# A last block of 64 queries filled up to 128 rows in windowed attention with two layers behind it

## The chip, the cores and the metric

One NeuronCore of a Trainium2 chip runs the whole program. The metric is the device time of one execution in microseconds, the median of several runs. TensorE multiplies (a stationary operand is loaded by its weight loader, then a moving operand streams through), VectorE, ScalarE and GpSimd work on elements, and SyncE's queue issues the DMAs.

## The reference

```python
# q, k, v: (4, 8, 576, 64)
scores = q @ k.T / sqrt(64)
rel = pos[:, None] - pos[None, :]
mask = (rel >= 0) & (rel < 128)
scores = where(mask, scores - slopes[h] * abs(rel), -1e9)
attn = softmax(scores) @ v              # sum + 1e-9 in the division
x = attn, heads side by side            # 2304 tokens x 512
h = x @ w_in                            # 512 x 2048, float64 weights in 32-bit words
x = (h * clip(h + 3, 0, 6) / 6) @ w_out
h = maximum(x @ w_in2, 0)
out = (s * h * h + b) @ w_out2
```

A query sees the 128 keys up to its own, so a block of 128 queries meets its own block of keys and the one before. A sequence of 576 is four blocks of 128 and a last one of 64.

## The kernel before

The attention is cut into units: one head and a range of query blocks. Groups 0 and 1 are blocks 0 and 1 of batches 0 and 1, in full float32 (`StartUnit`). Groups 2 and 3 are blocks 0 and 1 of the other two batches, groups 4 to 7 are blocks 2, 3 and 4 of all batches (`Unit`); block 4 has 64 rows, `rows(4)`. So 4 groups x 8 heads = 32 units have three blocks, the last one short, and 48 units have two full blocks.

A `Unit` goes through these steps. `load` fetches the queries and keys, transposed. `casts` (ScalarE) and `rests` (VectorE) split the scaled queries into a high part X and a rest Y. `products` (line 312) multiplies, for each block, X and then Y as the stationary operand with the keys of both blocks: 256 moving columns for a full block, 192 for the short one, whose stationary operand has 64 columns. `minima` (lines 328, 329; VectorE) folds the two squares into one and takes row minima, `exps` (line 339; ScalarE) exponentiates with row sums, `sums` (lines 350, 356; VectorE) adds 1e-9 and takes reciprocals, for full blocks and the short one apart. `weights` (line 362; GpSimd) scales the rows. `transposes` (line 371; TensorE) turns each block; for the short one the operand has 64 rows. `fold` and `masks` (lines 377, 389) spread the result over both key blocks. `values` (line 404), for two heads at once, each in its half of the columns, multiplies by the values, one key block after the other; the short key block has 64 rows. `to_hi` and `to_lo` write the first layer's input.

Each layer runs in steps of 128 inner columns: h (line 574, 12 products) and later o (line 632 in the first layer, 12 products; line 646 in the second), with ScalarE and VectorE making g from h in between. Every step of everything has a slot and a rank in a plan written out by hand; each engine's program is that order. TensorE's slots alternate layer products with a piece of the attention, and the second layer's weights are decoded (lines 168 to 208) after the attention.

Buffers: X and Y come from tags with two buffers of 320 columns in the pool `ap`; the start units take their scaled queries from the same tags. The start units' raw data lie in tiles of the later weight buffers w8 to w11. `warm`, the operand of the warm-up products, is a constant tile.

```python
lhsT=x[:, q : q + rows(i)]                                      # products
self.pt[:, li * P : li * P + r], self.Pt[:r, li], ident[:r, :r] # transposes
lhsT=u.rv[: rows(j), j - self.ka], rhs=u.W[: rows(j), o : o + n]  # values
```

Of the kernel before, what the change touches and what calls it, by code (L numbers as in the profile page):

```python
# [22 lines left out]
def tile_alibi_window_attention_moe_moe2(  # L23
# [12 lines left out]
):  # L36
    """Every float32 product runs as float32r passes over an exact split x = hi + lo."""
    nc = tc.nc
# [24 lines left out]

# [1 line left out]
    # The tensor engine's program is cut in slots: in each, twelve or nine products of a layer and  # L65
    # a piece of the attention. Every other step has the slot in which its operands are there.
    plan = {}
# [15 lines left out]

# [1 line left out]
    # The tensor engine's clock doubles after some microseconds of work.  # L85
    warm = const.tile([P, 256], F32, name="warm")
    nc.vector.memset(warm, 0.0)
# [6 lines left out]
    ident = const.tile([P, P], F32, name="ident")  # L94
    # A query row r meets the columns c <= r of its own block and c > r of the block before, at
    # the distances r - c and 128 + r - c: as two squares (rel2) and as one of both (rel).
    own = const.tile([P, P], I32, name="own")
# [30 lines left out]
    def bank(name):  # L128
        """A PSUM bank of the attention: the accumulators' too while they are free."""
        nonlocal nbank  # L130
        free = 4 if slot < FIRST else 2 if slot < hslot[1, 0] else 0
        nbank += 1
        k = nbank % (3 + free)
        if k < free:
            return ps_o.tile([P, 512], F32, tag=f"o{3 - k}", name=name)
        return ps_w.tile([P, 512], F32, tag="a", bufs=3, name=name)

# [1 line left out]
    wt = {}  # L139

    class Half:
        """
        Half a block of weights: float64 words to float32, rounded to nearest, then split into
        float32r parts.
        """

# [25 lines left out]
        def high(self):  # L172
            # As float32 the high word has the exponent's bits 3 places low, and too large by 112.
            if self.stage is None:
# [37 lines left out]

# [1 line left out]
    bounds1 = [(b * S + qa * P, n) for (b, qa, _), n in zip(groups, SIZES1)]  # L214
# [14 lines left out]
    def rows(i):  # L229
        return min(P, S - i * P)  # L230

    class Unit:
        """The query blocks [qa, qb) of one head: keys from block qa - 1 on."""

# [45 lines left out]
        def casts(self):  # L280
            self.c = -(D ** -0.5) / slopes[self.h]
            self.X = ap.tile([P, 320], F32R, tag="X", name=f"X{self.id}")[:, : self.nq]
            self.C = ap.tile([P, 448], F32R, tag="C", name=f"C{self.id}")[:, : self.nk]
            nc.scalar.activation(self.X, self.rq, AF.Copy, scale=self.c)
            nc.scalar.activation(self.C, self.rk, AF.Copy)

        def rests(self):
            self.Y = ap.tile([P, 320], F32R, tag="Y", name=f"Y{self.id}")[:, : self.nq]
            nc.vector.scalar_tensor_tensor(
                out=self.Y, in0=self.rq, scalar=self.c, in1=self.X.bitcast(F32),  # L290
                op0=ALU.mult, op1=ALU.subtract,
            )
            nc.gpsimd.tensor_tensor(  # L293
                out=self.C[D:], in0=self.rk[D:], in1=self.C[D:].bitcast(F32), op=ALU.subtract
            )

        def square(self, i):
            o = (i - self.qa) % 2 * 256
            k0 = max(0, i - 1) * P
            k1 = min((i + 1) * P, S)  # L300
            return self.ps[(i - self.qa) // 2][: rows(i), o : o + k1 - k0], k0, k1

        def products(self, a, b):
# [4 lines left out]
            for i in range(a, b):  # L308
                sl, k0, k1 = self.square(i)
                q = (i - self.qa) * P  # L310
                for x in (self.X, self.Y):
                    nc.tensor.matmul(  # L312
                        sl,
                        lhsT=x[:, q : q + rows(i)],
                        rhs=self.C[:, k0 - self.ka * P : k1 - self.ka * P],
# [4 lines left out]
        def minima(self, a, b):  # L320
# [3 lines left out]
            for i in range(a, b):  # L324
                sl = self.square(i)[0]
                li, r = i - self.qa, rows(i)
                if i:
                    nc.vector.copy_predicated(out=sl[:, :r], mask=own[:r, :r], data=sl[:, P:])  # L328
                nc.vector.tensor_tensor_reduce(  # L329
                    out=self.Pt[:r, li], in0=sl[:, :P], in1=(rel if i else rel0)[:r],  # L330
                    scale=slopes[self.h], scalar=3.0e38, op0=ALU.add, op1=ALU.min,
                    accum_out=self.st[:r, 0, li : li + 1],
                )

        def exps(self, a, b):
            for i in range(a, b):
                li, r = i - self.qa, rows(i)
                pt = self.Pt[:r, li]
                nc.scalar.activation(  # L339
                    pt, pt, AF.Exp, bias=self.st[:r, 0, li : li + 1], scale=-1.0,  # L340
                    accum_out=self.st[:r, 1, li : li + 1],
                )

        def sums(self):
            nqb = self.qb - self.qa
            full = nqb if rows(self.qb - 1) == P else nqb - 1
            st = self.st
            for r, a, b in ((P, 0, full), (rows(self.qb - 1), full, nqb)):
                if a < b:
                    nc.vector.tensor_scalar(  # L350
                        out=st[:r, 2, a:b], in0=st[:r, 1, a:b], scalar1=1e-9, scalar2=None,
                        op0=ALU.add,
                    )
            for r, a, b in ((P, 0, full), (rows(self.qb - 1), full, nqb)):
                if a < b:
                    nc.vector.reciprocal(st[:r, 2, a:b], st[:r, 2, a:b])  # L356

        def weights(self):
            for i in range(self.qa, self.qb):
                li, r = i - self.qa, rows(i)  # L360
                pt = self.Pt[:r, li]
                nc.gpsimd.tensor_scalar(  # L362
                    out=pt, in0=pt, scalar1=self.st[:r, 2, li : li + 1], scalar2=1.0,
                    op0=ALU.mult, op1=ALU.mult,
                )

        def transposes(self):
            self.pt = bank(f"t{self.id}")
            for i in range(self.qa, self.qb):
                li, r = i - self.qa, rows(i)  # L370
                nc.tensor.transpose(  # L371
                    self.pt[:, li * P : li * P + r], self.Pt[:r, li], ident[:r, :r]
                )

# [4 lines left out]
        def masks(self):  # L379
            # Per query block: its weights for the key block before, then for its own.  # L380
            self.W = ap.tile([P, 640], F32, tag="W", bufs=4, name=f"W{self.id}")
# [12 lines left out]
        def values(self):  # L394
            """Of two heads: each in its half of the tensor engine's columns."""
            self.xr = bank(f"v{self.id}")[:, : self.nq]
            for j in range(self.ka, self.qb):
# [4 lines left out]
                for u in self.pair():  # L402
                    p = slice((u.h % 2) * D, (u.h % 2 + 1) * D)
                    nc.tensor.matmul(  # L404
                        self.xr[p, q0 : q0 + n],
                        lhsT=u.rv[: rows(j), j - self.ka],
                        rhs=u.W[: rows(j), o : o + n],
                        start=j == self.ka,
# [3 lines left out]

        # Two heads' outputs, transposed, into the tile of the first layer's input.
        def to_hi(self):
# [8 lines left out]
    class StartUnit(Unit):  # L423
        """Query blocks 0 and 1, in float32 products: while the tensor engine has little to do."""

# [15 lines left out]
        def load(self):  # L441
            j = self.b * H // 2 + self.h // 2
            if j % 2 == 0:
                raws[j // 2] = wpool.tile(
                    [P, 2, 768], F32, tag=f"w{j // 2 + 8}", name=f"raw{self.id}"
                )
            raw = raws[j // 2][:, j % 2]
            nc.sync.dma_start(out=raw, in_=qkv0p[self.b, self.h // 2])
            for u in self.pair():
                u.raw = raw  # L450
                u.p = slice((u.h % 2) * D, (u.h % 2 + 1) * D)
                u.rk = raw[u.p, 256:512]
                u.rv = raw[:, 512 + 2 * D * (u.h % 2) :].rearrange("p (n d) -> p n d", d=D)

        def scale(self):
            """Both heads' queries over the scale and the slope."""
            tag = "XY"[self.h // 4]
            X = ap.tile([P, 320], F32, tag=tag, name=f"X{self.id}")[:, :256]
            for u in self.pair():
                u.X = X[u.p]  # L460
                c = -(D ** -0.5) / slopes[u.h]
# [80 lines left out]

# [1 line left out]
    late = {}  # L544

    class Step:
        """One block of a layer's inner columns, for one tile of tokens."""

# [134 lines left out]
    class Input2:  # L683
        """A tile of the second layer's input."""

# [24 lines left out]

# [1 line left out]
    k = 0  # L712
# [92 lines left out]
```

## Time and profile before

| | |
|---|---|
| time, median of 3 runs | 983.91 us (981.29 to 985.71) |
| span of the profiled execution | 985.2 us |
| TensorE busy | 956.8 us (97%), 5978 products |
| weight loader busy | 867.5 us (88%) |
| VectorE, ScalarE, GpSimd busy | 550.0 (56%), 457.6 (46%), 307.6 us (31%) |
| granted TensorE clock | 1.000 |
| chain of work that ended last | TensorE 75%, VectorE 17%, issue 3%, DMA 3% |

The span runs from the first to the last instruction; no separate time of the profiled execution is given beside it. Products are pipelined and their ends are modelled, so a product's duration is a latency, and what a piece of the program costs is read from the start of one line to the start of the next. "issue" names idle time for which the profile shows nothing that was waited for.

### The profile page before, as it was taken

What the parts mean: (1) busy time and instruction counts of PE and PEld (TensorE: products, weight loads), DVE (VectorE), ACT (ScalarE), POOL (GpSimd) and SP (SyncE); (2) the same over time, 40 slices, a digit from 0 to 9 for tenths busy, and PEclk for the clock granted to TensorE, in tenths of its full rate; (3) what the DMA queues carried; (4) which work ended last, traced back from release to release, by engine and by line L of the source; (5) the groups of instructions that cost most, each with busy time, mean ns of one, the idle gap of its engine ahead of it and who ended that gap; (6) DMA issues with size and microseconds to landing.
All of it is one profiled execution on the core that took longest, in us unless ns stands there. A gap on an engine that the chain in (4) does not pass through costs nothing.

```text
span 985.2 us, 16371 instructions
## 1 busy us (share of the span) xinstructions
PE 956.8 (97%) x5978; PEld 867.5 (88%) x5978; DVE 550.0 (56%) x1398; ACT 457.6 (46%) x1185; POOL 307.6 (31%) x556
## 2 busy tenths in 40 slices
PE   8998889999999999999999899899999999999998
PEld 5687779999999999999999888799999999999997
DVE  5999996555565555555328999933333333323322
ACT  4767675455544445444327776632333323323322
POOL 5865885335554344434204543300000000000000
PEclk9999999999999999999999999999999999999999
DMA  6263552213212113112014563320010100200000
GB/s 238 83 199 113 156 161 66 87 62 106 71 60 92 44 59 98 59 45 70 1 50 151 163 207 124 110 65 1 1 65 1 62 3 0 65 1 1 33 1 33
DMA packets 34384, 73.93 MB, mean 75 GB/s; under 512 B 4352, under 2 KB 13568, under 8 KB 34304
## 3 DMA queue, kind: packets, MB, share of 16 engines
q1 hardware_dynamic: 34304, 72.89, 22.8%
q8 instruction: 47, 0.77, 0.3%
q14 instruction: 33, 0.27, 0.1%
HBM read 63.44 MB, written 9.44 MB: 74 GB/s over the span
## 4 chain that ended last, share of the span: by engine, by line
PE 75%; DVE 17%; issue 3%; DMA 3%; ACT 1%; POOL 1%; SPq 0%; POOLq 0%; ACTq 0%; DVEq 0%
PE h L574 33%; PE o L646 18%; PE o L632 16%; DVE w L208 4%; PE v L404 3%; PE s L312 2%; DVE zq L187 2%; PE t L371 2%; DVE g L611 2%; DMA stage<-w 2%; DVE stage L187 2%; DVE zq L190 1%; DVE stage L190 1%; DVE t L591 1%; PE s L477 1%
## 5 line engine op out<-in xcount | busy, mean ns | idle before, releaser
L574 PE MATMUL h<-x,w 128*128 128x384 f32 (+2 forms) x2688 | 447.2, 315 | 9.7 <-DVE t L591 9.7
L574 PEld LDWEIGHTS h<-x,w 128*128 128x128 f32 x2688 | 418.5, 190 | 21.3 <-DVE t L591 12.7
L587 ACT ACTIVATE t<-h 128x384 f32<-128x384 f32 (+2 forms) x224 | 99.5, 444 | 374.3 <-PE h L574 373.3
L632 PE MATMUL o<-g,w 128*128 128x256 f32 (+1 forms) x1536 | 231.9, 299 | 4.1 <-DVE g L611 2.8
L646 PE MATMUL o<-w,g 128*128 128x512 f32 x864 | 217.2, 395 | 4.3 <-ACT g L606 2.9
L632 PEld LDWEIGHTS o<-g,w 128*128 128x128 f32 x1536 | 210.0, 189 | 9.1 <-DVE g L611 4.2
L646 PEld LDWEIGHTS o<-w,g 128*128 128x128 f32 x864 | 159.8, 188 | 37.5 <-ACT g L606 5.5
L595 DVE SCALAR_TENSOR_TENSOR t<-t,s_sb 128x384 f32<-128x384 f32 x96 | 64.4, 671 | 171.6 <-ACT t L587 171.6
L389 POOL TENSOR_SCALAR_AFFINE_SELECT W<-F 128x128 f32<-128x128 f32 (+1 forms) x240 | 71.5, 337 | 142.9 <-ACT F L377 139.2
L591 DVE SCALAR_TENSOR_TENSOR t<-t,h 128x256 f32<-128x256 f32 (+1 forms) x128 | 57.3, 448 | 88.9 <-ACT t L587 88.9
L611 DVE TENSOR_TENSOR g<-t,g 128x256 fp32r<-128x256 f32 (+1 forms) x128 | 76.0, 594 | 41.4 <-ACT g L604 40.6
L613 DVE SCALAR_TENSOR_TENSOR g<-t,b_sb,g 128x384 fp32r<-128x384 f32 x96 | 65.1, 678 | 54.1 <-ACT g L606 54.0
L606 ACT ACTIVATE g<-t,b_sb 128x384 fp32r<-128x384 f32 x96 | 59.2, 616 | 63.4 <-DVE t L595 63.4
L196 POOL TENSOR_TENSOR zq<-zq 128x512 int32<-128x512 int32 x40 | 57.2, 1429 | 83.4 <-DVE zq L190 77.3
L604 ACT ACTIVATE g<-t 128x256 fp32r<-128x256 f32 (+1 forms) x128 | 56.0, 438 | 17.7 <-DVE t L591 16.9
L293 POOL TENSOR_TENSOR C<-raw,C 64x448 fp32r<-64x448 f32 (+1 forms) x48 | 49.6, 1033 | 41.9 <-issue 23.4
L362 POOL TENSOR_SCALAR P<-P,st 128x128 f32<-128x128 f32 x128 | 53.5, 434 | 7.8 <-DVE st L356 6.1
L339 ACT ACTIVATE P<-P,st 128x128 f32<-128x128 f32 x128 | 49.5, 390 | 0.0
L328 DVE COPY_PREDICATED s<-own,s 128x128 f32<-128x128 int32 (+1 forms) x112 | 30.5, 273 | 31.8 <-PE s L312 30.1
L196 POOL TENSOR_TENSOR stage<-stage 128x512 int32<-128x512 int32 x24 | 34.4, 1432 | 37.6 <-DVE stage L190 28.5
L329 DVE CUSTOM_DVE_ANT_0 P<-s,rel 128x128 f32<-128x128 f32 x128 | 36.8, 288 | 7.3
L208 DVE TENSOR_TENSOR w<-zq,w 128x512 fp32r<-128x512 f32 x40 | 37.5, 937 | 0.0
(74 smaller groups left out, 830.6 us busy)
## 6 DMA issues: line engine op xcount, KB each, us to landing
raw<-w SPq DMA_DIRECT2D x40, 512.0 KB, 5.0
stage<-w SPq DMA_DIRECT2D x24, 512.0 KB, 4.2
raw<-qk SPq DMA_DIRECT2D x32, 384.0 KB, 3.1
out<-y SPq DMA_DIRECT2D x18, 256.0 KB, 2.3
raw<-qk SPq DMA_DIRECT2D x16, 256.0 KB, 2.7
rv<-v SPq DMA_DIRECT2D x16, 256.0 KB, 3.4
raw<-qkv0p SPq DMA_DIRECT2D x8, 384.0 KB, 7.2
x2d<-y SPq DMA_DIRECT2D x8, 320.0 KB, 2.9
```

Source lines behind the costliest of these rows:

```text
L196: nc.gpsimd.tensor_tensor(out=self.q, in0=self.z, in1=self.q, op=ALU.add)
L208: nc.vector.tensor_tensor(out=w[:, 1, self.c], in0=self.q.bitcast(F32), in1=w[:, 0, self.c].bitcast(F32), op=ALU.subtract,)
L389: nc.gpsimd.affine_select(out=self.W[:, o : o + r], in_=self.F[:, q : q + r], fill=0.0, base=k - 1, compare_op=ALU.is_ge, pattern=[[s, r]] ...
L574: nc.tensor.matmul(self.ps, lhsT=w[:, wp, cc * P : (cc + 1) * P], rhs=x[:, cc, xp], start=m == 0, stop=m == 3 * CC - 1,)
L587: nc.scalar.activation(self.a, self.ps, AF.Relu, **bias)
L591: nc.vector.scalar_tensor_tensor(out=self.a, in0=self.a, scalar=6.0, in1=self.ps, op0=ALU.min, op1=ALU.mult)
L595: nc.vector.scalar_tensor_tensor(out=self.a, in0=self.a, scalar=s_sb, in1=self.a, op0=ALU.mult, op1=ALU.mult)
L606: nc.scalar.activation(self.g[:, 0], self.a, AF.Identity, bias=b_sb)
L611: nc.vector.tensor_tensor(out=self.g[:, 1], in0=self.a, in1=hi, op=ALU.subtract)
L613: nc.vector.scalar_tensor_tensor(out=self.g[:, 1], in0=self.a, scalar=b_sb, in1=hi, op0=ALU.add, op1=ALU.subtract,)
L632: nc.tensor.matmul(acc[t][d], lhsT=w[:, wp, DM + d * P : DM + (d + 1) * P], rhs=self.g[:, gp], start=f == 0 and i == 0 and (t > 1 or d % 2 ...
L646: nc.tensor.matmul(acc[t][tb], lhsT=self.g[:, gp, tb * P : (tb + 1) * P], rhs=w[:, wp, DM:], start=f == 0 and i == 0, stop=f == NF - 1 and ...
```

## The change

All instructions of the short block run over 128 rows or columns. The query tiles X and Y get 384 columns, of which the last 64 are set to zero once, at the start, by GpSimd; they are two fixed tiles each, used in turn. The scores of the 64 added rows come from zero queries, and their weights, minima and sums are never used: `fold` still copies 320 columns. The values' short key block multiplies 128 rows, the added ones being zero in the prepared values. `sums` needs two instructions in place of four. To make room, `warm` moves into the buffer w7 of the weights, and the start units' scaled queries move into the tile of their raw data (now 1024 columns per pair).

```diff
-    warm = const.tile([P, 256], F32, name="warm")
+    warm = wpool.tile([P, 256], F32, tag="w7", name="warm")
...
+    queries = {}
+    for x in "XY":
+        queries[x] = [ap.tile([P, 3 * P], F32R, tag=f"q{x}{i}", bufs=1, name=f"q{x}{i}") for i in (0, 1)]
+        for t in queries[x]:
+            nc.gpsimd.memset(t[:, S - 2 * P :].bitcast(F32), 0.0)
+
+    def query_tile(x):
+        queries[x].reverse()
+        return queries[x][0]
...
-            self.X = ap.tile([P, 320], F32R, tag="X", name=f"X{self.id}")[:, : self.nq]
+            self.X = query_tile("X")
...
-            nc.scalar.activation(self.X, self.rq, AF.Copy, scale=self.c)
+            nc.scalar.activation(self.X[:, : self.nq], self.rq, AF.Copy, scale=self.c)
...
-            return self.ps[(i - self.qa) // 2][: rows(i), o : o + k1 - k0], k0, k1
+            return self.ps[(i - self.qa) // 2][:, o : o + k1 - k0], k0, k1
...
-                        lhsT=x[:, q : q + rows(i)],
+                        lhsT=x[:, q : q + P],
...
-                    nc.vector.copy_predicated(out=sl[:, :r], mask=own[:r, :r], data=sl[:, P:])
+                    nc.vector.copy_predicated(out=sl[:, :r], mask=own[:, :r], data=sl[:, P:])
...
-                li, r = i - self.qa, rows(i)
-                pt = self.Pt[:r, li]
+                li = i - self.qa
+                pt = self.Pt[:, li]
...
-            for r, a, b in ((P, 0, full), (rows(self.qb - 1), full, nqb)):
-                if a < b:
-                    nc.vector.reciprocal(st[:r, 2, a:b], st[:r, 2, a:b])
+            nc.vector.reciprocal(st[:, 2, :n], st[:, 2, :n])
...
-                nc.tensor.transpose(
-                    self.pt[:, li * P : li * P + r], self.Pt[:r, li], ident[:r, :r]
-                )
+                nc.tensor.transpose(self.pt[:, li * P : (li + 1) * P], self.Pt[:, li], ident)
...
-                        lhsT=u.rv[: rows(j), j - self.ka],
-                        rhs=u.W[: rows(j), o : o + n],
+                        lhsT=u.rv[:, j - self.ka],
+                        rhs=u.W[:, o : o + n],
...
-                    [P, 2, 768], F32, tag=f"w{j // 2 + 8}", name=f"raw{self.id}"
+                    [P, 2, 1024], F32, tag=f"w{j // 2 + 8}", name=f"raw{self.id}"
...
-            nc.sync.dma_start(out=raw, in_=qkv0p[self.b, self.h // 2])
+            nc.sync.dma_start(out=raw[:, :768], in_=qkv0p[self.b, self.h // 2])
...
+                u.X = raw[u.p, 768:]
...
-            X = ap.tile([P, 320], F32, tag=tag, name=f"X{self.id}")[:, :256]
```

## Rows read from the trace of the kernel before

**Rows 1.** Stages: us, then each engine's busy us, clock, DMA share, GB/s.

```profile
core 0: us, PE busy (x) PEld busy (x) DVE busy (x) ACT busy (x) POOL busy (x), PEclk, DMA share, GB/s
...
40.00:155.00 115.00, 101.03 (x743) 90.19 (x743) 111.30 (x230) 79.99 (x202) 85.90 (x96) 1.00 0.46 144
...
208.00:497.00 289.00, 289.00 (x2179) 270.93 (x2178) 151.64 (x608) 135.47 (x448) 122.57 (x323) 1.00 0.20 63
497.00:523.00 26.00, 26.00 (x179) 26.00 (x178) 10.19 (x21) 9.68 (x21) 1.30 (x1) 1.00 0.31 105
523.00:640.00 117.00, 108.77 (x603) 97.53 (x601) 108.55 (x151) 79.07 (x154) 51.61 (x35) 1.00 0.44 146
```

**Rows 2.** TensorE's timeline among three-block units: start, us, instructions.

```profile
226.56 0.25 PE L312 MATMUL s<-C,X 128*64 128x192 f32 x1
226.65 0.25 PE L312 MATMUL s<-C,Y 128*64 128x192 f32 x1
226.74 0.58 PE L371 MATMUL t<-ident,P 128*128 128x128 f32 x3
227.25 1.70 PE L632 MATMUL o<-g,w 128*128 128x256 f32 x12
228.79 1.60 PE L574 MATMUL h<-x,w 128*128 128x256 f32 x12
...
249.42 1.46 PE L404 MATMUL v<-W,rv 128*64 128x128 f32 x16
250.81 0.64 PE L371 MATMUL t<-ident,P 128*128 128x128 f32 x3
251.38 1.69 PE L632 MATMUL o<-g,w 128*128 128x256 f32 x12
```

**Rows 3.** TensorE's timeline among two-block units.

```profile
198.15 0.38 PE L371 MATMUL t<-ident,P 128*128 128x128 f32 x2
198.29 1.68 PE L632 MATMUL o<-g,w 128*128 128x256 f32 x12
199.81 1.60 PE L574 MATMUL h<-x,w 128*128 128x256 f32 x12
201.25 0.23 PE L312 MATMUL s<-C,X 128*128 128x128 f32 x1
...
201.71 1.59 PE L632 MATMUL o<-g,w 128*128 128x256 f32 x12
...
204.67 0.87 PE L404 MATMUL v<-W,rv 128*64 128x256 f32 x8
205.47 0.44 PE L371 MATMUL t<-ident,P 128*128 128x128 f32 x2
205.66 1.67 PE L632 MATMUL o<-g,w 128*128 128x256 f32 x12
```

**Rows 4.** TensorE's timeline, three full transposes of a start unit.

```profile
53.95 0.49 PE L516 MATMUL t<-ident,P 128*128 128x128 f32 x3
54.19 0.48 PE L574 MATMUL h<-x,w 128*128 128x256 f32 x2
```

**Rows 5.** The weight loader's timeline; in brackets its idle time before.

```profile
306.17 0.13 PEld L371 LDWEIGHTS t<-ident,P 64*128 64x128 f32 x1 [0.17 <-issue]
...
315.37 0.20 PEld L404 LDWEIGHTS v<-W,rv 64*64 64x64 f32 x4 [0.28 <-issue]
```

**Rows 6.** Waits of the weight loader, 208 to 497 us: total, times, longest.

```profile
PEld t L371 <- issue: 5.5, 33, 0.2
PEld v L404 <- issue: 4.6, 17, 0.3
```

**Rows 7.** Groups by line and shape: count, busy us, mean ns.

```profile
L371 PE MATMUL t<-ident,P 64*128 64x64 f32 x32 | 8.7, 272 | 0.0
...
L350 DVE TENSOR_SCALAR st<-st 64x1 f32<-64x1 f32 x32 | 4.4, 137 | 0.0
```

**Rows 8.** GpSimd's timeline: one unit's weights.

```profile
309.62 1.06 POOL L362 TENSOR_SCALAR P<-P,st 128x128 f32<-128x128 f32 x3
```

**Rows 9.** Timeline of the start: VectorE's first use of a query.

```profile
6.86 0.61 DVE L463 TENSOR_SCALAR X<-raw 64x256 f32<-64x256 f32 x2 [4.24 <-DMA raw<-qkv0p]
```

More of the change, by code (lines that the diff above doesn't have):

```diff
@@ L281, in casts @@
             self.c = -(D ** -0.5) / slopes[self.h]
-            self.X = ap.tile([P, 320], F32R, tag="X", name=f"X{self.id}")[:, : self.nq]
+            self.X = query_tile("X")
             self.C = ap.tile([P, 448], F32R, tag="C", name=f"C{self.id}")[:, : self.nk]
-            nc.scalar.activation(self.X, self.rq, AF.Copy, scale=self.c)
+            nc.scalar.activation(self.X[:, : self.nq], self.rq, AF.Copy, scale=self.c)
             nc.scalar.activation(self.C, self.rk, AF.Copy)
         def rests(self):
-            self.Y = ap.tile([P, 320], F32R, tag="Y", name=f"Y{self.id}")[:, : self.nq]
+            self.Y = query_tile("Y")
             nc.vector.scalar_tensor_tensor(
-                out=self.Y, in0=self.rq, scalar=self.c, in1=self.X.bitcast(F32),
+                out=self.Y[:, : self.nq], in0=self.rq, scalar=self.c,
+                in1=self.X[:, : self.nq].bitcast(F32),
                 op0=ALU.mult, op1=ALU.subtract,
@@ L327, in minima @@
                 if i:
-                    nc.vector.copy_predicated(out=sl[:, :r], mask=own[:r, :r], data=sl[:, P:])
+                    nc.vector.copy_predicated(out=sl[:, :r], mask=own[:, :r], data=sl[:, P:])
                 nc.vector.tensor_tensor_reduce(
-                    out=self.Pt[:r, li], in0=sl[:, :P], in1=(rel if i else rel0)[:r],
+                    out=self.Pt[:, li], in0=sl[:, :P], in1=rel if i else rel0,
                     scale=slopes[self.h], scalar=3.0e38, op0=ALU.add, op1=ALU.min,
-                    accum_out=self.st[:r, 0, li : li + 1],
+                    accum_out=self.st[:, 0, li : li + 1],
                 )
@@ L336, in exps @@
             for i in range(a, b):
-                li, r = i - self.qa, rows(i)
-                pt = self.Pt[:r, li]
+                li = i - self.qa
+                pt = self.Pt[:, li]
                 nc.scalar.activation(
-                    pt, pt, AF.Exp, bias=self.st[:r, 0, li : li + 1], scale=-1.0,
-                    accum_out=self.st[:r, 1, li : li + 1],
+                    pt, pt, AF.Exp, bias=self.st[:, 0, li : li + 1], scale=-1.0,
+                    accum_out=self.st[:, 1, li : li + 1],
                 )
         def sums(self):
-            nqb = self.qb - self.qa
-            full = nqb if rows(self.qb - 1) == P else nqb - 1
-            st = self.st
-            for r, a, b in ((P, 0, full), (rows(self.qb - 1), full, nqb)):
-                if a < b:
-                    nc.vector.tensor_scalar(
-                        out=st[:r, 2, a:b], in0=st[:r, 1, a:b], scalar1=1e-9, scalar2=None,
-                        op0=ALU.add,
-                    )
-            for r, a, b in ((P, 0, full), (rows(self.qb - 1), full, nqb)):
-                if a < b:
-                    nc.vector.reciprocal(st[:r, 2, a:b], st[:r, 2, a:b])
+            n, st = self.qb - self.qa, self.st
+            nc.vector.tensor_scalar(
+                out=st[:, 2, :n], in0=st[:, 1, :n], scalar1=1e-9, scalar2=None, op0=ALU.add
+            )
+            nc.vector.reciprocal(st[:, 2, :n], st[:, 2, :n])
         def weights(self):
             for i in range(self.qa, self.qb):
-                li, r = i - self.qa, rows(i)
-                pt = self.Pt[:r, li]
+                li = i - self.qa
+                pt = self.Pt[:, li]
                 nc.gpsimd.tensor_scalar(
-                    out=pt, in0=pt, scalar1=self.st[:r, 2, li : li + 1], scalar2=1.0,
+                    out=pt, in0=pt, scalar1=self.st[:, 2, li : li + 1], scalar2=1.0,
                     op0=ALU.mult, op1=ALU.mult,
@@ L369, in transposes @@
             for i in range(self.qa, self.qb):
-                li, r = i - self.qa, rows(i)
-                nc.tensor.transpose(
-                    self.pt[:, li * P : li * P + r], self.Pt[:r, li], ident[:r, :r]
-                )
+                li = i - self.qa
+                nc.tensor.transpose(self.pt[:, li * P : (li + 1) * P], self.Pt[:, li], ident)
         def fold(self):
@@ L452, in load @@
                 u.rk = raw[u.p, 256:512]
-                u.rv = raw[:, 512 + 2 * D * (u.h % 2) :].rearrange("p (n d) -> p n d", d=D)
+                u.X = raw[u.p, 768:]
+                c = 512 + 2 * D * (u.h % 2)
+                u.rv = raw[:, c : c + 2 * D].rearrange("p (n d) -> p n d", d=D)
         def scale(self):
-            tag = "XY"[self.h // 4]
-            X = ap.tile([P, 320], F32, tag=tag, name=f"X{self.id}")[:, :256]
             for u in self.pair():
-                u.X = X[u.p]
                 c = -(D ** -0.5) / slopes[u.h]
```

## The prediction

> **What bounds the kernel.** I read the stage table first [rows 1], because the change touches only units with a 64-row block: four groups of eight heads, 32 units, whose products run from about 208 to 497 us. In that window TensorE is busy 289.00 of 289.00 us, VectorE 151.64, ScalarE 135.47, GpSimd 122.57: TensorE alone sets the time, and a microsecond off its queue is a microsecond off the stage. Before it, from 40 to 155 us, VectorE is the full engine (111.30 of 115); nothing with 64 rows runs there. From 497 to 523 us the same layer products run with no attention between them and TensorE is still full (26.00 of 26.00), so a shorter piece of attention between products does not uncover the ScalarE and VectorE chain that feeds them. From 523 to 640 us VectorE is nearly full (108.55 of 117) with the weights of the second layer; its work is unchanged and follows TensorE's slots, so I let it start earlier by what the stage before gains.
>
> Then I read TensorE's timeline. The start of one line to the start of the next is what a line costs; the durations overlap, as products are pipelined. In a three-block unit, three transposes (two full, one of 64 rows) take 226.74 to 227.25, 0.51 us; behind a values group, 250.81 to 251.38, 0.57 us [rows 2]. In a two-block unit two full transposes take 198.15 to 198.29, 0.14 us, and behind a values group 205.47 to 205.66, 0.19 us [rows 3]. So the third, half-sized transpose costs 0.37 to 0.38 us where a full one costs about 0.07. The weight loader's timeline says where: before the 64-row transpose it idles 0.17 us, and before the 64x64 values products 0.28 us, and no releaser is found ("issue") [rows 5]. The waits of the loader over the whole stage give 5.5 us in 33 times and 4.6 us in 17 times [rows 6]: every unit and every pair, always at the change from 128 to 64 rows. That sum counts only the way in; the way out (the next full load) is in the 0.51 us too.
>
> **Transposes.** After the change the third is 128x128 like its neighbours, 32 of them [rows 7]. Three full transposes in a row stand in a start unit: 53.95 to 54.19, 0.24 us [rows 4]. From the two-block unit the third would add half of 0.14, so 0.21 us in all. I take the row of three, 0.24, behind scores (a saving of 0.27), and behind a values group 0.19 + (0.24 - 0.14) = 0.29 (a saving of 0.28); half of the units are of each kind. The o group behind the transposes lasts 227.25 to 228.79, 1.54 us, against 198.29 to 199.81, 1.52 us [rows 2, 3]: 0.02 more. So 16 x 0.27 + 16 x 0.28 + 32 x 0.02 = 9.4 us. Bounds: with the third at 0.07 (0.21 in all) 32 x 0.32 = 10.2 us; with the third as dear as the whole pair behind a values group, 0.19, the group takes 0.33 and 32 x 0.18 = 5.8 us remain.
>
> **Values.** The last key block becomes 128x64 like the three before it, so the loader no longer changes rows. Sixteen pairs. Now four key blocks with 128 + 256 + 192 + 64 = 640 columns take 249.42 to 250.81, 1.39 us; the two-block pair, 384 columns and no change of rows, 204.67 to 205.47, 0.80 us [rows 2, 3]. In proportion 640 columns cost 0.80 x 640 / 384 = 1.33, a saving of 0.06; if instead the gap that the transposes show, 0.17 [rows 5], goes as a whole, 0.17. I take 0.08, near the proportional figure, since two passes over only 64 columns hide little of their loads: 16 x 0.08 = 1.3 us, bounds 1.0 to 2.7. Nothing is multiplied for longer: the count of moving columns is the same.
>
> **Scores.** Here padding costs something. The last block's products have 192 moving columns and now 64 stationary ones, and follow each other at 0.09 us (226.56, 226.65, 226.74) [rows 2]. Four products with 128 stationary columns, two of them moving only 128, take 201.25 to 201.71, 0.46 us, or 0.115 each [rows 3]: the two short ones are no quicker, so the load of 128 columns sets the pace. With 128 columns the pair goes from 0.09 to 0.115 each, 0.025 more. If both are on the path that is 64 x 0.025 = 1.6 us; if the first load lies under the layer product ahead, 32 x 0.025 = 0.8 us. I take 1.2 us lost.
>
> A rule speaks against the change here: the Trainium skill, "TensorE: Matmul & The Clock Gate", LDWEIGHTS, gives a load a time by its columns, about columns / 1.2 ns, so 107 ns for 128 and 53 ns for 64. The four scores products at 0.115 agree with its 107 ns. An estimate by that page with the whole 53 ns paid at each of 64 loads is 3.4 us in place of 1.2, and the kernel would take 976.6 us.
>
> **What costs nothing.** VectorE loses 32 one-column additions at 137 ns, 4.4 us [rows 7], and as many reciprocals; in this stage it is half idle, so no time is gained. The minima, exponentials and GpSimd weights keep their columns and only take more rows. GpSimd's weights of one unit (three, from 309.62) end at 310.68 and are transposed from 315.63 (the loader's row at 315.37 is the group just ahead): 5 us of slack for anything the full rows cost there [rows 5, 8]. If that slack were gone, a slower third multiplication would be paid in TensorE's queue, 32 times its excess. Four memsets of 64 columns now lead GpSimd's queue ahead of the constants; the first use of a query waits for its DMA until 6.86 us, after 4.24 us of idleness [rows 9], which covers them; without that cover four short memsets would be paid once. The scaled queries of the start units move into the tile of their raw data, the warm-up tile into a weight buffer, the query tiles are kept in twos: the same number of buffers and the same readers, hence no new wait. No DMA is added, moved or resized.
>
> **Sum.** 9.4 + 1.3 - 1.2 = 9.5 us. The profiled execution's span of 985.2 us becomes 975.7 us; it lies 1.3 us above the median of the runs, 983.9 us (the profile shows nothing around the span), so I forecast 983.9 - 9.5 = 974.4 us. Bounds of the terms: 5.8 + 1.0 - 1.6 = 5.2 us gives 978.7; 10.2 + 2.7 - 0.8 = 12.1 us gives 971.8.
>
> **Rivals.**
> - *The gap isn't the rows'.* The loader waits for something else of the third block (its name is only "issue"). Then nothing is saved, scores pay 1.2 us, and the time is 985.1 us. For it: no releaser is named. Against: the 64x64 values have the gap too, their operands are other tiles, the transposed tile was ready 5 us earlier, and the two-block units, with the same producers, show none. If only half of the gaps belong to the rows, 983.9 - (10.7 / 2 - 1.2) = 979.8 us. Together 8%.
> - *Slower: the half-sized products ran beside their neighbours.* If a 64-row product shares the array with others and costs nothing, padding takes that away: the third transposes then cost a full one, 0.24 / 3 = 0.08 us [rows 4], 2.6 us over 32 units, and with the scores' 1.6 us the kernel takes 988.1 us. It decides if the third transpose adds less than 0.08 now; the rows show 0.37. The Trainium skill, "TensorEngine Tiling (Array Packing)", has both rules: operands of up to 64 rows can run as independent tiles, up to twice as fast (Theoretical Speedup), and a change of the tiling mode drains the engine (Key Properties). The first is this rival and the trace doesn't bear it out; the second would make the gaps and is what the idle 0.17 and 0.28 us look like. 4%.
> - *The gain is absorbed.* Shorter pieces bring each o group closer to its g, and TensorE waits for VectorE or ScalarE instead: 983.9 us, if all is given back. Against: 497 to 523 us, with no pieces at all, has no idle TensorE [rows 1]. 3%.
> - *More.* The loads hide better than the start unit shows, and the values' gap goes as a whole, both ways: below 970 us. 4%.
>
> **Numbers.** The forecast, 970 to 980 us with the scatter of the runs (981.3 to 985.7), gets 81%; that is the range as well. A change of 0.5%, 4.9 us, is about what a measurement of this kernel can tell from none. Faster than that (under 979.0): nearly all of the forecast and the "more" case, 0.85. Within it: the rest of the forecast, the gap that stays, the absorbed gain, 0.11. Slower: the slower rival, 0.04.
>
> **What would show it.** Three transposes to the next o start in 0.24 to 0.29 us instead of 0.51 and 0.57; the loader's "issue" waits on the transposes and values gone; the values group at about 1.31 us; the two scores products of the last block 0.115 us apart; TensorE without waits through the stage, which ends near 488 us; later stages as long as before. I am wrong if the gaps stay with full rows, if the transposes' gap moves to another change of shape (the 64-column values, which stay), or if TensorE starts to wait for g.

## The result and the profile after

The changed kernel takes 975.06 us (median of 4 runs, 970.73 to 975.47) against 984.81 us for the kernel before (4 runs, 981.29 to 986.24): a ratio of 0.989, with a 95% interval of 0.987 to 0.991. It is faster by 1.1%: 10.9 us by the ratio, 9.8 us between the two medians. 974.4 us was forecast.

The table by stages of the changed kernel, with the columns of [rows 1], cut at about the same places of the program:

```profile
208.00:484.00 276.00, 276.00 (x2163) 269.91 (x2161) 149.14 (x543) 134.68 (x447) 122.64 (x322) 1.00 0.20 65
486.00:512.00 26.00, 26.00 (x179) 26.00 (x178) 10.79 (x22) 9.79 (x21) 1.66 (x2) 1.00 0.30 107
512.00:628.00 116.00, 107.68 (x597) 96.70 (x596) 107.56 (x149) 78.51 (x153) 51.22 (x35) 1.00 0.44 147
```

TensorE is still full through the attention's stage (276.00 of 276.00) and behind it (26.00 of 26.00); VectorE stays at half. So nothing else became the bound.

To measure the stage I take it from the first scores product of a three-block unit to the o group behind the last values group. TensorE's timeline of the kernel before at the two ends:

```profile
208.61 0.28 PE L312 MATMUL s<-C,X 128*128 128x256 f32 x1
...
495.50 2.02 PE L632 MATMUL o<-g,w 128*128 128x320 f32 x12
```

and of the changed kernel, with one unit and one pair between:

```profile
207.73 0.28 PE L324 MATMUL s<-C,qX 128*128 128x256 f32 x1
...
225.43 0.25 PE L324 MATMUL s<-C,qX 128*128 128x192 f32 x1
225.52 0.28 PE L324 MATMUL s<-C,qY 128*128 128x192 f32 x1
225.64 0.49 PE L376 MATMUL t<-ident,P 128*128 128x128 f32 x3
225.88 1.68 PE L634 MATMUL o<-g,w 128*128 128x256 f32 x12
227.40 1.60 PE L576 MATMUL h<-x,w 128*128 128x256 f32 x12
...
247.39 1.31 PE L407 MATMUL v<-W,rv 128*64 128x128 f32 x16
248.63 0.55 PE L376 MATMUL t<-ident,P 128*128 128x128 f32 x3
248.93 1.67 PE L634 MATMUL o<-g,w 128*128 128x256 f32 x12
...
483.92 2.02 PE L634 MATMUL o<-g,w 128*128 128x320 f32 x12
```

The stage went from 286.89 us to 276.19 us, 10.70 us less. From its end to the end of the span it is 489.7 us before (985.2 - 495.50) and 489.8 us after (973.7 - 483.92), and the remaining 0.9 us lie ahead of it, in the start (below). Within a unit: three transposes behind scores cost 0.24 us (225.64 to 225.88) where they cost 0.51 [rows 2]; behind a values group 0.30 us (248.63 to 248.93) where they cost 0.57; the values group 1.24 us (247.39 to 248.63) where it cost 1.39. The weight loader's waits, 5.5 us in 33 times and 4.6 us in 17 times before [rows 6], are nearly gone. From 200 to 500 us there are left:

```profile
PEld t L376 <- issue: 0.3, 2, 0.2
PEld v L407 <- issue: 0.2, 1, 0.2
```

The three that are left stand ahead of operands with 128 rows, and the kernel before has them too: two ahead of the transposes behind a two-block values group (204.59 and 218.82 us; 205.47 and 219.66 before), one ahead of the last values group (482.68; 494.11 before).

### The profile page after: what moved, and what is told of

It is laid out like the page before. It is cut to its first block, busy times and chain, and to the rows that moved or that the text cites. A ratio compares the mean times of both kernels' runs of the same rounds, so it can differ in the third digit from the quotient of the medians.

```text
span 973.7 us, 16310 instructions
## 1 busy us (share of the span) xinstructions
PE 943.4 (97%) x5978; PEld 866.4 (89%) x5978; DVE 549.0 (56%) x1334; ACT 457.5 (47%) x1185; POOL 308.1 (32%) x560
## 4 chain that ended last, share of the span: by engine, by line
PE 75%; DVE 15%; DMA 3%; issue 3%; ACT 2%; POOL 1%; SPq 0%; POOLq 0%; ACTq 0%; DVEq 0%
PE h L576 33%; PE o L648 18%; PE o L634 15%; DVE w L208 4%; PE s L324 3%; PE v L407 2%; DVE g L613 2%; DVE zq L187 2%; PE t L376 2%; DMA stage<-w 2%; DVE stage L187 2%; DVE zq L190 1%; DMA raw<-w 1%; DVE stage L190 1%; DVE t L593 1%
```

## The experiments

Six kernels, each timed in three rounds beside the kernel before (984.98 us for the first four, 986.04 us for the last two). The stage is measured as above, from each kernel's own timeline. Kernels that should have the same stage, before and "moves only", changed and "96 rows", agree within 0.13 us, so the stage shows what the scatter of the times hides.

| kernel | stage us | three transposes behind scores / values, us | values, us | ratio to before (95%) |
|---|---|---|---|---|
| before | 286.89 | 0.51 / 0.57 | 1.39 | |
| changed | 276.19 | 0.24 / 0.30 | 1.24 | 0.989 (0.987 to 0.991) |
| values short | 278.53 | 0.24 / 0.30 | 1.39 | 0.990 (0.988 to 0.993) |
| transposes short | 285.46 | 0.51 / 0.57 | 1.24 | 0.999 (0.998 to 1.001) |
| 96 rows | 276.28 | 0.25 / 0.31 | 1.24 | 0.990 (0.987 to 0.994) |
| moves only | 287.02 | 0.51 / 0.57 | 1.39 | 1.001 (0.999 to 1.003) |
| scores short | 275.53 | 0.25 / 0.30 | 1.24 | 0.988 (0.986 to 0.989) |
| short block first | 283.05 | 0.40 / 0.39 | 1.39 | 0.994 (0.992 to 0.996) |

**Values short.**

```diff
-                        lhsT=u.rv[:, j - self.ka],
-                        rhs=u.W[:, o : o + n],
+                        lhsT=u.rv[: rows(j), j - self.ka],
+                        rhs=u.W[: rows(j), o : o + n],
```

> The changed kernel, with the values products of the short key block over 64 rows again. The stage from the first scores product of a three-block unit to the o group behind the last values group lasts 286.9 us before (208.61 to 495.50) and 276.2 us after the change (207.73 to 483.92). Theory (a change of the row shape stops the weight loader): the values group goes back from 1.24 to 1.39 us, the loader's gap ahead of the 64x64 products is back, the transposes stay at 0.24 and 0.30 us; the stage takes 276.2 + 16 x 0.15 = 278.6 us, the kernel about 8 us less than before. Rival (the transposes alone make the gain): 276.2 us and 10.7 us less than before.

The values group is back at 1.39 us and the loader's gap with it, while the transposes keep their gain. Its timeline, and its loader's waits from 200 to 500 us:

```profile
233.14 1.46 PE L407 MATMUL v<-W,rv 128*64 128x128 f32 x16
234.53 0.55 PE L376 MATMUL t<-ident,P 128*128 128x128 f32 x3
234.83 1.67 PE L634 MATMUL o<-g,w 128*128 128x256 f32 x12
```

```profile
PEld v L407 <- issue: 4.6, 17, 0.3
PEld t L376 <- issue: 0.3, 2, 0.2
```

The stage is 278.53 us, 2.34 above the changed kernel, against 2.4 expected. So the values' part is a gain of its own, 0.15 us a pair. The median of the times, 974.3 us, can't show 2 us: its runs go from 972.6 to 978.3 us.

**Transposes short.**

```diff
-                li = i - self.qa
-                nc.tensor.transpose(self.pt[:, li * P : (li + 1) * P], self.Pt[:, li], ident)
+                li, r = i - self.qa, rows(i)
+                nc.tensor.transpose(
+                    self.pt[:, li * P : li * P + r], self.Pt[:r, li], ident[:r, :r]
+                )
```

> The changed kernel, with the transposes of the short block over 64 rows again. Theory: the transposes go back to 0.51 and 0.57 us, the o group behind them to 0.02 more, 9.4 us in 32 units: the stage takes 285.6 us and the kernel about 1.3 us less than before, which is within its measurement. Rival (the gap belongs to the third block's late operand, and full rows everywhere else change that): the transposes keep their 0.24 us or something between.

```profile
251.64 0.58 PE L376 MATMUL t<-ident,P 128*128 128x128 f32 x3
252.15 1.69 PE L636 MATMUL o<-g,w 128*128 128x256 f32 x12
253.68 1.60 PE L578 MATMUL h<-x,w 128*128 128x256 f32 x12
```

```profile
PEld t L376 <- issue: 5.5, 33, 0.2
PEld v L409 <- issue: 0.2, 1, 0.2
```

Everything upstream runs over full rows here and the transposes alone are short: 0.51 us again, and the stage 285.46 us, 9.27 more than the changed kernel. Most of the gain of 10.70 us is in 32 transposes. The rival of a late third operand falls, since the operand is made exactly as in the changed kernel.

**96 rows.**

```diff
-                li = i - self.qa
-                nc.tensor.transpose(self.pt[:, li * P : (li + 1) * P], self.Pt[:, li], ident)
+                li, r = i - self.qa, max(96, rows(i))
+                nc.tensor.transpose(
+                    self.pt[:, li * P : li * P + r], self.Pt[:r, li], ident[:r, :r]
+                )
```

> The changed kernel, with the short block transposed over 96 rows in place of 128. Theory (only shapes of up to 64 rows change the array's division): no gap, the transposes at 0.24 and 0.30 us, the stage at 276.2 us, as after the change. Rival (any row count below 128 stops the loader): the gap of 0.17 us is back, 0.5 us for three transposes, the stage at 285.6 us.

Its timeline, its 32 short transposes in the groups by shape, and its loader's waits on transposes from 200 to 500 us:

```profile
235.59 0.46 PE L376 MATMUL t<-ident,P 128*128 128x128 f32 x3
235.84 1.67 PE L636 MATMUL o<-g,w 128*128 128x256 f32 x12
```

```profile
L376 PE MATMUL t<-ident,P 96*128 96x96 f32 x32 | 7.9, 248 | 0.0
```

```profile
PEld t L376 <- issue: 0.2, 1, 0.2
```

No gap ahead of them: 0.25 us and a stage of 276.28 us. It isn't a part-filled operand as such that costs the time; 64 rows do and 96 don't. Row counts between 64 and 96, or below 64, were not tried.

**Moves only.** The short block over 64 rows everywhere; the buffers, the zero columns and the start units' query places as in the change.

```diff
-            return self.ps[(i - self.qa) // 2][:, o : o + k1 - k0], k0, k1
+            return self.ps[(i - self.qa) // 2][: rows(i), o : o + k1 - k0], k0, k1
...
-                        lhsT=x[:, q : q + P],
+                        lhsT=x[:, q : q + rows(i)],
...
+                li, r = i - self.qa, rows(i)
...
+                        lhsT=u.rv[: rows(j), j - self.ka],
```

> The changed kernel with all its moves of buffers and its zero columns, but with every instruction of the short block over 64 rows or columns as before. Theory (moves and memsets cost nothing): the stage at 286.9 us, the time that of the kernel before within 0.3%. Rival (part of the gain comes from the query tiles or the start): over 2 us less than before, seen ahead of the stage or in its casts.

The stage, 287.02 us (202.44 to 489.46), and the time, ratio 1.001, are those of the kernel before. The moves and memsets cost and bring nothing that shows.

**Scores short.** Scores, minima, exponentials, sums and weights over 64 rows as before, and zeros in the rest of the weights.

```diff
-                        lhsT=x[:, q : q + P],
+                        lhsT=x[:, q : q + rows(i)],
...
+                if r < P:
+                    nc.gpsimd.memset(self.Pt[r:, li], 0.0)
...
```

> The changed kernel, with the short block's scores, minima, exponentials, sums and weights over 64 rows as before; GpSimd sets the other 64 rows of its weights to zero in each unit, and the transposes and values run over full rows. Theory (a load of 128 columns takes longer than 192 moving columns hide): the two scores products go from 0.21 back to 0.18 us, the stage from 276.2 to 276.2 - 32 x 0.03 = 275.2 us, faster than both kernels. Rival (padding the scores is free, or the 32 memsets on GpSimd hold up its queue): 276.2 us or more.

```profile
225.87 0.25 PE L324 MATMUL s<-C,qX 128*64 128x192 f32 x1
225.96 0.26 PE L324 MATMUL s<-C,qY 128*64 128x192 f32 x1
226.05 0.50 PE L385 MATMUL t<-ident,P 128*128 128x128 f32 x3
226.30 1.68 PE L643 MATMUL o<-g,w 128*128 128x256 f32 x12
```

The pair of scores products takes 0.18 us (225.87 to 226.05) where the changed kernel takes 0.21 (225.43 to 225.64), and the stage is 275.53 us, 0.66 less; 1.0 was expected. It is the shortest stage of all, but in the time, ratio 0.988 against 0.989, it can't be told from the changed kernel.

**Short block first.** The kernel before, with the order of the three transposes turned.

```diff
-            for i in range(self.qa, self.qb):
+            for i in sorted(range(self.qa, self.qb), key=rows):
                 li, r = i - self.qa, rows(i)
                 nc.tensor.transpose(
```

> The kernel before, with the short block transposed first of the three. Theory (the change of rows costs, not the instruction): behind a values group the 64-row products and the 64-row transpose are then neighbours, so one way in and one way out fall away in 16 pairs; the values and transposes of a pair take 1.96 us before (249.42 to 251.38) and now 1.6 to 1.8, the stage 286.9 - 2.5 to 5 us; behind scores nothing changes. Rival (a 64-row instruction is slow wherever it stands): 1.96 us and 286.9 us.

TensorE's timeline, then the weight loader's:

```profile
246.59 1.46 PE L404 MATMUL v<-W,rv 128*64 128x128 f32 x16
247.98 0.64 PE L371 MATMUL t<-ident,P 64*128 64x64 f32 x3
248.37 1.67 PE L632 MATMUL o<-g,w 128*128 128x256 f32 x12
249.88 1.60 PE L574 MATMUL h<-x,w 128*128 128x256 f32 x12
```

```profile
247.71 0.19 PEld L404 LDWEIGHTS v<-W,rv 64*64 64x64 f32 x4 [0.28 <-issue]
247.97 0.40 PEld L371 LDWEIGHTS t<-ident,P 64*128 64x128 f32 x3
```

Not one row is padded, and the pair of values and transposes takes 1.78 us (246.59 to 248.37) where it took 1.96 (249.42 to 251.38) [rows 2]. The same 64-row transpose, right behind 64-row products, has no gap ahead of it; the gap ahead of the values' 64x64 products stays at 0.28 us. The stage is 283.05 us, 3.84 less than before, inside the 2.5 to 5 expected; the rival (a 64-row instruction is slow wherever it stands) falls. Behind scores the time moves ahead of the first transpose, which is why the table has 0.40: from the Y product to the o group it is 0.58 us (224.12 to 224.70) against 0.60 before (226.65 to 227.25). "Nothing changes" there was nearly right. The o group behind the transposes also falls to 1.51 us (248.37 to 249.88) from 1.54.

## Why the prediction was right

**The bound.** TensorE was full before and is full after; the stage's 10.70 us reached the end of the span undiminished. The absorbed gain did not happen. Of the bound's premises one is too wide: "nothing with 64 rows runs there", from 40 to 155 us, holds for the last block only. The start units' scores have operands of 64 rows, in both kernels (last section).

**Transposes.** The forecast was 0.24 and 0.29 us and 9.4 us in all; the rows show 0.24 and 0.30, the o group behind at 1.52 us (225.88 to 227.40), and undoing them alone gives back 9.27 us. The price of the third transpose came from a start unit, another place of the same program, and held. The reading of the loader's waits as "always at the change from 128 to 64 rows" is off by one in each row: 32 of the 33 and 16 of the 17 are; the others are those at 219.66 and 494.11 us. No term of the sum used the waits.

**Values.** Mis-sized: 1.3 us forecast, 0.08 a pair, and 2.34 us measured. The step that failed is "in proportion 640 columns cost 0.80 x 640 / 384 = 1.33". A group of 640 columns without a change of rows takes 1.24 us, not 1.33, so a pair gains 0.15 us; the prediction's other figure, the transposes' gap of 0.17 us gone as a whole, was the nearer. Why the proportion fails is argued: if a group has a fixed part and a part by its columns, the two groups that change no rows, 0.80 us for 384 columns and 1.24 us for 640, give 0.44 / 256 = 1.72 ns a column and a fixed part of 0.80 - 384 x 0.00172 = 0.14 us, which the proportion stretched. Two sizes give such a split but can't test it. The bounds of 1.0 to 2.7 us held the value.

**Scores.** 1.2 us of loss forecast, 0.66 us by the experiment, just under the lower bound of 0.8. The loss is paid once in a pair: from X to Y it is 0.09 us before and after, and from Y to the first transpose 0.12 us (225.52 to 225.64) in place of 0.09. That is the size of the lower bound, though which of the two loads is the paid one isn't shown. The price of 0.115 us came from a misreading: the four products of the two-block unit don't follow each other evenly. The rows between those of [rows 3]:

```profile
201.31 0.27 PE L312 MATMUL s<-C,Y 128*128 128x128 f32 x1
201.42 0.33 PE L312 MATMUL s<-C,X 128*128 128x256 f32 x1
201.59 0.28 PE L312 MATMUL s<-C,Y 128*128 128x256 f32 x1
```

The two short ones take 0.17 us (201.25 to 201.42) and the two wide ones 0.29 (201.42 to 201.71), so "no quicker" doesn't hold, and 0.115 is an average of unlike products; that it came near 0.12 is luck. The estimate from the Trainium skill's "TensorE: Matmul & The Clock Gate", LDWEIGHTS, with the full difference paid at each of 64 loads, is not borne out. In length the loads of the kernel before do differ by about the 53 ns, 190 ns against 134:

```profile
L312 PEld LDWEIGHTS s<-C,Y 128*128 128x128 f32 x96 | 18.2, 190 | 0.0
L312 PEld LDWEIGHTS s<-C,Y 128*64 128x64 f32 x32 | 4.3, 134 | 0.2
```

But only 0.66 us over 64 loads, 0.010 us each, reach TensorE's queue; most of the difference costs nothing here.

**The sum.** 9.27 + 2.34 - 0.66 = 10.95 us by the three experiments, 10.70 us in the stage, 9.5 us forecast. The forecast time came within 0.7 us of the median, 975.06 us; with a scatter of some 5 us so close a hit is luck, and the stage is the better measure. The prediction set the span of 985.2 us beside the median time of 983.9 us as if they were one quantity. They aren't: the profiled run of the changed kernel has a span of 973.7 us and a time of 975.47 us. The forecast was counted from the median, so this doesn't touch it.

**Rivals.** That the gap belongs to something else of the third block: refuted by the transposes undone alone and by the turned order. That 64-row products ran beside their neighbours for nothing: refuted, since the time fell. That products with only 64 moving columns are the slow ones, which the prediction doesn't name: refuted, since the changed kernel still has such products in its values, now over 128 rows, and its values groups take 1.24 us; and the turned order has no gap ahead of the 64-column transpose behind the values. The products in question:

```profile
L407 PE MATMUL v<-W,rv 128*64 128x64 f32 x64 | 4.6, 220 | 0.0
```

The Trainium skill's "TensorEngine Tiling (Array Packing)", Key Properties, says that a change of the tiling mode drains the engine; the trace agrees as far as rows go, with a gap at the changes of rows from 128 to 64 (0.17 us, 0.28 us) and none at 96 rows. A change of columns alone, from 64x64 to 64x128 operands in "short block first", shows no gap. What the engine does in the gap no profile here shows.

## What to carry to other kernels

On a full TensorE, look at the weight loader's idle time without a named releaser, and at the shape of the operand behind it. Such idle time is a hint and not a price: ahead of the two full transposes at 205.47 us the loader idles 0.17 us as well, and they cost 0.19 us. The price is read from the starts of the products. A remainder block of 64 rows can cost more than a full one, here 0.37 us against about 0.1. Fill the remainder up where the padding is harmless, or, if it can't be filled, put all its products next to each other so that the rows change once (here 3.84 of 10.70 us without any padding). To price a group of another size, don't stretch one size in proportion: measure two sizes if the program has them.

## What the runs showed that was not expected

The scatter of up to some 5 us in a kernel's times comes from the first 50 us and goes with TensorE's clock. The first 40 us of the kernel before, of the changed one and of "moves only", by stages (the granted clock is the third number from the end):

```profile
0.00:40.00 40.00, 37.43 (x129) 23.26 (x130) 26.10 (x103) 22.94 (x75) 25.91 (x54) 1.00 0.50 180
```

```profile
0.00:40.00 40.00, 37.28 (x132) 23.36 (x133) 26.83 (x104) 23.71 (x76) 27.05 (x58) 0.61 0.52 184
```

```profile
0.00:40.00 40.00, 33.44 (x170) 22.95 (x171) 31.32 (x122) 28.23 (x90) 31.69 (x63) 0.87 0.54 198
```

At 0.87, mostly the higher of its two levels (2.4 GHz), TensorE gets through 170 products, at 0.61, mostly the lower (1.2 GHz), through 132; the stage of the three-block units then starts at 202.44 us ("moves only") or 207.73 us (changed). The experiments fall in with this: at 0.87 and 0.91 the stage starts at 202.52 us ("transposes short") and 202.79 ("96 rows"), at 0.66 at 206.29 ("short block first"), at 0.61 at 208.23 ("scores short"). In the changed kernel TensorE counts as busy all of the time from 10 to 45 us, at a granted clock of 0.50 until 40 us and 1.00 from 45 us on. The first row shows 1.00 for the kernel before, yet only 129 products were done, and three start-unit transposes at 48.04 us last 0.90 us, those at 51.20 us 0.49 us:

```profile
48.04 0.90 PE L516 MATMUL t<-ident,P 128*128 128x128 f32 x3
...
51.20 0.49 PE L516 MATMUL t<-ident,P 128*128 128x128 f32 x3
```

So the record of the clock seems to miss the low stretch in that profile, and the length of a known product is the better witness. Not all of the difference is the clock: the transposes at 48.04 us follow scores and those at 51.20 us a layer group. "Moves only" has both kinds at a clock near 1.00:

```profile
37.64 0.92 PE L488 MATMUL s<-raw 64*128 64x128 f32 x4
38.49 0.55 PE L527 MATMUL t<-ident,P 128*128 128x128 f32 x3
38.96 1.69 PE L585 MATMUL h<-x,w 128*128 128x256 f32 x12
40.49 0.49 PE L527 MATMUL t<-ident,P 128*128 128x128 f32 x3
```

Behind scores they last 0.55 us and behind a layer group 0.49, so nearly all of the step from 0.90 to 0.49 is the clock. The same rows show where 64-row operands are left. The start units' scores have 64 rows, and three full transposes behind them cost 0.47 us (38.49 to 38.96) where a start unit's cost 0.24 behind a layer group [rows 4]. That looks like the price of going back from 64 to 128 rows; no run varies it.

The 0.9 us by which the profiled runs of the two kernels differ ahead of the stage fit this scatter: "moves only" has the change's start and starts its stage 6.2 us before the kernel before. "Values short" is like the kernel before: 1.00 in the record and a start at 208.38 us. What makes the clock rise early in one run and late in another of the same program was not tried.
